# Pooled attention feeding a GELU MLP: v over 128 partitions, and a first batch by two head pairs

## The chip, the cores and the metric

The kernel runs on one core of a Trainium2 chip. The time is the device time of the program in microseconds, the median of several runs. The core's engines are TensorE (PE), VectorE (DVE), ScalarE (ACT), GpSimd (POOL) and SyncE (SP), each with its own instruction queue; SP, ACT and POOL issue transfers.

## The reference

Eight batches, eight heads, 576 positions of 64 columns. k and v are averaged over groups of eight positions (72 rows are left), and q attends to them; the result of all heads, 4608 rows of 512 columns, goes through two weight matrices with a tanh GELU between them. Everything is given and returned in f32.

```python
k_p = k.reshape(B, H, Sp, pool, D).mean(axis=3)          # Sp = 576 / 8 = 72
v_p = v.reshape(B, H, Sp, pool, D).mean(axis=3)
attn = softmax(scale * q @ k_p^T)
x = (attn @ v_p), heads side by side                     # (4608, 512)
out = gelu_tanh(x @ w_in) @ w_out                        # w_in (512, 2048), w_out (2048, 512)
```

## The kernel before, in words

The order of all instructions is written out by hand. The MLP works in nine groups `g` of 512 rows of x (`NG`), the attention in eight batches of 576 rows; while group g is worked on, batch `nb = g + 1` is prepared in the gaps. The work of one group has two parts.

In the first, `p1_mm` (L280) multiplies x by w_in: 16 blocks `fo` of 128 columns of the hidden layer, four matmuls `ko` each, 512 columns moving; `gelu` (L285) takes each block out of PSUM on ACT. `plan` (L369 and L372) says after which `fo` the preparation of batch nb is put: pooling of k (`k_steps`, three additions on DVE at L145), pooling of v (`v_steps`, by halves of four heads), the transposition of k on PE with its copies on DVE (`trans_k`, L168), and for batch 1 that of q (`trans_q`, L184). Later batches have q transposed by a DMA (`trans_q_dma`, L198).

In the second, `p2_mm` (L290) multiplies by w_out, 64 matmuls, and between them, at the positions `pos`, stands the attention of batch nb: `qk` (L208) makes scores with pooled positions on partitions, `expo` takes the exponential on ACT, `av` (L224) multiplies by pooled v. In `av` a weight tile holds 64 columns of v and 64 columns of the value 8, so that one matmul yields both the output and the sum of the softmax. `norm` (L241) makes the reciprocal as Exp(-Ln) on ACT, `mult` (L252) multiplies on DVE into `xT`. `store` (L294) copies a finished bank of output to SBUF on DVE and stores it from SP.

Group 0 has no group before it, so batch 0 is prepared and attended at the start, by itself (L305 to L348). There the sums of the softmax have matmuls of their own (`ones`, L234), and a unit of work is one pair of heads and one half `c` of the 576 positions: eight `av`, `norm` and `mult` in a row. Matmuls of `idle` (`spin`, L309) stand between the real ones. The first matmuls of group 0 are made early for the 288 columns of the first half (`early`, `take`), and completed later for the other 224.

Loads: k of batch 0 comes in two halves from SP and ACT, its last rows behind the second; v comes from SP by halves of heads, with pooled positions on 72 partitions (64 and 8). q, w_in, w_out and all later k and v are loaded by POOL, and q, w_in and w_out become bf16 on the way. w_in is loaded by four blocks of 512 columns, the first two at once, the others behind batch 1's k and q. `gate` (L358) is a copy on POOL that waits for a transposed q before later loads are issued. PSUM has eight banks, which `h_bank`, `o_bank` and the arguments `bank` share out.

Of the kernel before, what the change touches and what calls it, by code (L numbers as in the profile page):

```python
# [18 lines left out]
def kernel(  # L19
# [29 lines left out]
    kvp = ctx.enter_context(tc.tile_pool(name="kvp", bufs=2))  # L49
# [12 lines left out]
    vs, qs = {}, {}  # L62
    kts = [consts.tile([128, KR + 1, 512], F32, name=f"kt{i}") for i in range(2)]

    def load_k(b, engs):
        rows = k[b].rearrange("h (j l) d -> (h j) (l d)", l=8)
        main = rows[0:128 * KR].rearrange("(p r) c -> p r c", r=KR)
        n = KR // len(engs)
        for i, eng in enumerate(engs):
            eng.dma_start(out=kts[b % 2][:, i * n:(i + 1) * n], in_=main[:, i * n:(i + 1) * n])  # L70
        engs[-1].dma_start(out=kts[b % 2][64:128, KR], in_=rows[128 * KR:])

    def load_v(b, eng, h0=0, h1=H):
        if b not in vs:
            vs[b] = kvp.tile([Sp, H, 512], F32, name="vt")
        rows = v[b, h0:h1].rearrange("h (j l) d -> j h (l d)", l=8)

        for j0, j1 in ((0, 64), (64, Sp)) if eng is nc.sync else ((0, Sp),):
            eng.dma_start(out=vs[b][j0:j1, h0:h1], in_=rows[j0:j1])  # L79
# [8 lines left out]
    w_in_b = consts.tile([128, KO, DF], BF16, name="w_in_b")  # L88
    w_out_b = consts.tile([128, FO, DM], BF16, name="w_out_b")
    w_in_v = moe_w_in.rearrange("(ko p) f -> p ko f", p=128)  # L90
    w_out_v = moe_w_out.rearrange("(fo p) d -> p fo d", p=128)
# [4 lines left out]
    load_v(0, nc.sync, 0, 4)  # L96
    load_v(0, nc.sync, 4, 8)
# [4 lines left out]
    def load_w_in(i):  # L102
        nc.gpsimd.dma_start(out=w_in_b[:, :, i * 512:(i + 1) * 512], in_=w_in_v[:, :, i * 512:(i + 1) * 512])

    load_w_in(0)
    load_w_in(1)


    xT = consts.tile([128, KO, N], BF16, name="xT")

    kTs = [consts.tile([128, 2, H, Sp], BF16, name=f"kT{i}") for i in range(2)]
    kps = [consts.tile([128, KR + 2, D], BF16, name=f"kp{i}") for i in range(2)]

    vps = [consts.tile([Sp, PR, 2, 2, D], BF16, name=f"vp{i}") for i in range(2)]

    vz = consts.tile([Sp, PR, 2, 2, D], BF16, name="vz")
    ones = consts.tile([Sp, 2, 2, D], BF16, name="ones")
    gate = consts.tile([1, 2], BF16, name="gate")
# [4 lines left out]
    nc.vector.memset(kTs[0], 0.0)  # L123
    nc.vector.memset(vz, 0.0)
    nc.vector.memset(ones, 0.0)
    nc.vector.memset(ones[:, 0, 0], 8.0)
    nc.vector.memset(ones[:, 1, 1], 8.0)
    nc.gpsimd.memset(kTs[1], 0.0)
    nc.gpsimd.memset(kps[1], 0.0)
    nc.gpsimd.memset(kts[1][0:64, KR], 0.0)  # L130
    nc.gpsimd.memset(vps[0], 8.0)
    nc.gpsimd.memset(vps[1], 8.0)

    load_k(1, [nc.gpsimd])
    load_q(1)
    load_w_in(2)
    load_w_in(3)
    for i in range(4):
        nc.gpsimd.dma_start(out=w_out_b[:, 4 * i:4 * i + 4, :], in_=w_out_v[:, 4 * i:4 * i + 4, :])

# [13 lines left out]
    def v_steps(b, hf):  # L154
        t = vs[b][:, hf * 4:(hf + 1) * 4]

        def s3():
            w = (vps[b % 2] if b else vz)[:, 2 * hf:2 * hf + 2]
            for e in range(2):
                add(w[:, :, e, e, :], t[:, e::2, 0:64], t[:, e::2, 64:128])  # L160

        return [lambda: add(t[:, :, 0:256], t[:, :, 0:256], t[:, :, 256:512]),
                lambda: add(t[:, :, 0:128], t[:, :, 0:128], t[:, :, 128:256]), s3]
# [4 lines left out]
    def trans_k(b, bank, odd_eng=None):  # L168
        tp = half_bank(bank)[:, 0:(KR + 1) * 128].rearrange("p (r c) -> p r c", c=128)
        kf = kps[b % 2].rearrange("p r d -> p (r d)")  # L170
        for r in range(KR + 1):
            nc.tensor.transpose(out=tp[:, r, :], in_=kf[:, r * D:r * D + 128], identity=identb)  # L172
        tp = tp[0:D]
        n7 = (H - 1) * KH
        for e in range(2):
            copy = nc.scalar.copy if e and odd_eng is nc.scalar else nc.vector.tensor_copy
            o = kTs[b % 2][e * 64:(e + 1) * 64, e]
            copy(out=o[:, 0:H - 1].rearrange("p h (j r) -> p h j r", r=KR),  # L178
                 in_=tp[:, 0:KR, 0:n7].rearrange("p r (h j) -> p h j r", j=KH))
            copy(out=o[:, H - 1, 0:(128 - n7) * KR].rearrange("p (j r) -> p j r", r=KR),  # L180
                 in_=tp[:, 0:KR, n7:128].rearrange("p r j -> p j r"))
            copy(out=o[:, H - 1, (128 - n7) * KR:], in_=tp[:, KR, 64:128])

    def trans_q(b, i, t0, n, bank, eng):  # L184
        if b not in qTs:
            qTs[b] = bp.tile([128, 2, TP, 128], BF16, name="qT")
        tp = half_bank(bank)[:, 0:n * 128].rearrange("p (t c) -> p t c", c=128)
        for x in range(n):
            nc.tensor.transpose(out=half_bank(bank)[:, x * 128:(x + 1) * 128],  # L189
                                in_=qs[b][:, i, (t0 + x) * 128:(t0 + x + 1) * 128],  # L190
                                identity=identb)
        o = qTs[b][:, i, t0:t0 + n]
        if eng is nc.scalar:
            nc.scalar.copy(out=o, in_=tp)
        else:
            nc.vector.tensor_copy(out=o, in_=tp)

# [9 lines left out]

    def qk(b, c, pr, bank):  # L208
        for e in range(2):
            h = 2 * pr + e  # L210
            nc.tensor.matmul(out=PS[:Sp, bank + e, :CH].rearrange("j (t p) -> j t p", p=32),  # L211
                             lhsT=kTs[b % 2][:, c, h, :],
# [3 lines left out]
    def expo(b, c, pr, bank):  # L216
        e = ep.tile([Sp, 2, CH], BF16, name="e", bufs=8)
        nc.scalar.activation(out=e, in_=PS[:Sp, bank:bank + 2, :CH], func=ACT.Exp, scale=1.0 / 64.0)  # L218
        es[b, c, pr] = e

    def flat(w):
        return w.rearrange("j a d -> j (a d)")

    def av(b, c, pr, bank):  # L224

        e = es.pop((b, c, pr))
        for x in range(2):
            if b:  # L230
                nc.tensor.matmul(out=PS[:, bank + x, :CH], lhsT=flat(vps[b % 2][:, pr, x]),  # L231
                                 rhs=e[:, x, :], start=True, stop=True)
            else:
                for y in range(2):  # L234
                    w = vz[:, pr, y] if x else ones[:, y]
                    nc.tensor.matmul(out=PS[:, bank + 1 - x, :CH], lhsT=flat(w), rhs=e[:, y, :],  # L236
                                     start=(y == 0), stop=(y == 1))
# [3 lines left out]
    def norm(b, c, pr, bank):  # L241
        ld = ep.tile([128, CH], F32, name="ld")
        if b:
            nc.scalar.activation(out=ld[0:64], in_=PS[64:128, bank, :CH], func=ACT.Ln)  # L244
            nc.scalar.activation(out=ld[64:128], in_=PS[0:64, bank + 1, :CH], func=ACT.Ln)  # L245
        else:
            nc.scalar.activation(out=ld, in_=PS[:, bank + 1, :CH], func=ACT.Ln)  # L247
# [4 lines left out]
    def mult(b, c, pr, bank):  # L252
        rc = rcs.pop((b, c, pr))
        col = b * S + c * CH
        for x in range(2 if b else 1):
            rows = slice(x * 64, (x + 1) * 64) if b else slice(0, 128)
            nc.vector.tensor_tensor(out=xT[rows, pr, col:col + CH], in0=PS[rows, bank + x, :CH],  # L257
                                    in1=rc[rows], op=ALU.mult)

# [9 lines left out]
    def h_bank(g, fo):  # L269
        x, y = x_bank(g), 1 - x_bank(g)  # L270
        if fo == 4:
# [8 lines left out]
    def p1_mm(g, fo, ko, c0=0, c1=GROUP):  # L280
        r0 = g * GROUP
        nc.tensor.matmul(out=PS[:, h_bank(g, fo), c0:c1], lhsT=w_in_b[:, ko, fo * 128:(fo + 1) * 128],  # L282
# [22 lines left out]
    act_set(EXP_SET)  # L305
    for s in k_steps(0):
        s()

    def spin(n):  # L309

        for _ in range(n):
            nc.tensor.matmul(out=PS[:, 7, :], lhsT=idle[:, 0:128], rhs=idle, start=True, stop=True)  # L312

    def scores(b, c, pr, bank):
        qk(b, c, pr, bank)
        expo(b, c, pr, bank)

    spin(16)
    trans_q(0, *QG[0], 5, nc.scalar)
    trans_q(0, *QG[1], 6, nc.scalar)  # L320
    spin(4)
    trans_k(0, 4, nc.scalar)
    trans_q(0, *QG[2], 5, nc.vector)
    trans_q(0, *QG[3], 6, nc.vector)
    spin(2)
    for i, (c, pr) in enumerate(((0, 0), (0, 1), (1, 0), (1, 1), (0, 2), (0, 3), (1, 2), (1, 3))):
        if i:
            spin(1)
        scores(0, c, pr, (2, 0)[i % 2])
    for hf in range(2):  # L330
        for s in v_steps(0, hf):
            s()

    early = [(fo, ko) for ko in range(KO) for fo in range(4)]
    take = (0, 0, 0, 0, 0, 4, 6, 6)
    for i, (c, pr) in enumerate(ORDER):
        bank = (4, 6, 0, 2, 4, 6, 4, 6)[i]
        av(0, c, pr, bank)
        norm(0, c, pr, bank)
        mult(0, c, pr, bank)  # L340
        if i == 3:

            vs[1] = kvp.tile([Sp, H, 512], F32, name="vt")
            nc.vector.memset(vs[1][:, 0, 0:1], 0.0)  # L344
            load_v(1, nc.sync)
        for fo, ko in early[:take[i]]:
            p1_mm(0, fo, ko, 0, CH)
        early = early[take[i]:]  # L348


    for g in range(NG):
        nb = g + 1 if g + 1 < B else None
        act_set(GELU_SET)
        if g + 2 < B:
# [5 lines left out]
            load_v(g + 2, nc.gpsimd)  # L360
# [3 lines left out]
        if nb is not None:  # L364
            kk = k_steps(nb)
            v0, v1 = v_steps(nb, 0), v_steps(nb, 1)
            tk = [lambda: trans_k(nb, 4)]
            if g:
                plan = {2: kk[:1], 3: kk[1:], 7: v0[:1], 8: v0[1:], 9: tk, 11: v1[:1], 12: v1[1:]}  # L369
            else:  # L370
                tq = [lambda a=a, i=i: trans_q(nb, *a, 4 + i, nc.vector) for i, a in enumerate(QG)]
                plan = {0: kk, 4: tk, 6: tq[:1], 7: tq[1:2], 8: tq[2:3], 9: tq[3:], 10: v0, 12: v1}  # L372
# [5 lines left out]
        if g == 0:  # L378
            first = [(fo, ko, CH) for ko in range(KO) for fo in range(4)]
        else:  # L380
            late = 3
            rest = [fo for fo in range(4) if fo != late]
            first = [(fo, ko, 0) for ko in range(2) for fo in rest]
            first += [(late, 0, 0), (late, 1, 0)]
            first += [(fo, ko, 0) for ko in (2, 3) for fo in rest + [late]]
# [73 lines left out]
```

The softmax here doesn't subtract the row's maximum and nothing guards it: scores larger than these inputs give would overflow.

## Time and profile before

| | |
|---|---|
| median of 11 runs | 311.59 us (310.74 to 312.5) |
| the profiled execution | 311.74 us, span 310.0 us |
| mean granted TensorE clock | 0.992 |
| matmuls of `p1_mm` and `p2_mm` | 580 and 560 recorded, 375 and 379 ns each |
| exp of scores, 72x576 | 644 ns |
| Ln and Exp of `norm` in batch 0, 128x288 | 398 and 442 ns |
| HBM read, written | 36.70 MB, 9.44 MB |

The span is the time from the first to the last instruction of one profiled execution; around it lie the 1.7 us to its own time. Matmuls overlap, so the mean duration of one (379 ns) is not the distance between two: 31 of them follow each other in 6.94 us. A wait is put down to what ended it.

### The profile page before, as it was taken

The numbers are of one execution on the slowest core, as the hardware profiler recorded it, in microseconds if no ns is written. First come the engines' busy times: TensorE is split into PE (matmuls) and PEld (weight loads), VectorE is DVE, ScalarE is ACT, GpSimd is POOL, SyncE is SP. The second block draws the span as 40 slices with busy tenths as digits, with TensorE's granted clock in tenths as the row PEclk, the third lists the DMA queues.
The fourth block names the chain that finished last, engine by engine and source line by source line (L and its number), as shares of the span: only waits on it lengthen the run. The fifth ranks groups of instructions, "written<-read, shape, count | busy, mean of one in ns | idle before, by whom it ended". The sixth has DMA issues, their size and how long they took to land.

```text
span 310.0 us, 4249 instructions
## 1 busy us (share of the span) xinstructions
PE 297.1 (96%) x1516; PEld 150.3 (48%) x1545; DVE 157.2 (51%) x304; ACT 220.9 (71%) x414; POOL 30.8 (10%) x54
## 2 busy tenths in 40 slices
PE   6788999999999999999999999999999999999994
PEld 2455555445554455445544554455445544444441
DVE  3766636647668455854495358636772640020011
ACT  1686579877997799778987898689868987306500
POOL 8520000300201200030003000200000000000000
PEclk9988999999999999999999999999999999999998
DMA  7999995894995982588358826482101220121022
GB/s 225 236 279 248 185 193 116 271 220 83 261 220 113 239 183 63 112 232 174 79 110 226 188 71 95 164 184 71 41 0 33 49 56 0 36 68 34 2 68 69
DMA packets 32701, 41.05 MB, mean 132 GB/s; under 512 B 17608, under 2 KB 21704, under 8 KB 31784
## 3 DMA queue, kind: packets, MB, share of 16 engines
q0 software_dynamic: 10160, 24.26, 35.1%
q1 hardware_dynamic: 22200, 15.74, 21.7%
q10 hardware_dynamic: 320, 0.79, 0.8%
q8 instruction: 12, 0.20, 0.2%
q14 instruction: 9, 0.07, 0.1%
HBM read 36.70 MB, written 9.44 MB: 149 GB/s over the span
## 4 chain that ended last, share of the span: by engine, by line
PE 89%; DMA 4%; DVE 3%; ACT 1%; issue 1%; SPq 1%; DVEq 0%; ACTq 0%
PE PS L291 39%; PE PS L282 39%; PE PS L211 5%; PE PS L231 4%; DMA vt<-in_v_dram 4%; DVE kt L145 1%; PE PS L172 1%; SPq L79 1%; DVE vt L145 1%; DVE kT L178 0%; PE PS L236 0%; ACT rc L249 0%; PE PS L189 0%; ACT ld L247 0%; DVE osb L296 0%
## 5 line engine op out<-in xcount | busy, mean ns | idle before, releaser
L291 PE MATMUL PS<-w_out_b,gT 128*128 128x512 bf16 x560 | 133.7, 379 | 0.8
L282 PE MATMUL PS<-xT,w_in_b 128*128 128x512 bf16 (+2 forms) x580 | 129.2, 375 | 0.9 <-DVE vt L344 0.3
L288 ACT ACTIVATE gT<-PS 128x512 bf16<-128x512 f32 x144 | 81.3, 603 | 47.1 <-PE PS L282 46.9
L282 PEld LDWEIGHTS <-w_in_b 128*128 128x128 bf16 x592 | 57.7, 98 | 65.4 <-issue 2.0
L291 PEld LDWEIGHTS <-gT 128*128 128x128 bf16 x576 | 56.0, 97 | 56.9 <-issue 0.4
L296 DVE COPY osb<-PS 128x512 f32<-128x512 f32 x36 | 24.9, 692 | 94.9 <-PE PS L291 94.9
L257 DVE TENSOR_TENSOR xT<-PS,rc 64x288 bf16<-64x288 f32 (+1 forms) x120 | 54.5, 455 | 31.3 <-ACT rc L249 23.8
L218 ACT ACTIVATE e<-PS 72x576 bf16<-72x576 f32 x64 | 40.7, 644 | 8.0 <-PE PS L211 7.2
L145 DVE TENSOR_TENSOR vt<-vt 72x1024 f32<-72x1024 f32 (+1 forms) x32 | 30.5, 953 | 6.7 <-DMA vt<-in_v_dram 5.9
L249 ACT ACTIVATE rc<-ld 128x288 f32<-128x288 f32 x64 | 28.3, 443 | 2.6 <-DVE xT L257 0.6
L211 PE MATMUL PS<-qT,kT 128*72 128x288 bf16 x128 | 26.1, 286 | 0.4 <-ACT e L218 0.3
L244 ACT ACTIVATE ld<-PS 64x288 f32<-64x288 f32 x56 | 22.8, 407 | 1.3
L245 ACT ACTIVATE ld<-PS 64x288 f32<-64x288 f32 x56 | 22.5, 402 | 1.4
L263 ACT ACT_TABLE_LOAD x17 | 21.8, 1283 | 2.1 <-issue 1.8
L231 PE MATMUL PS<-e,vp 72*128 72x288 bf16 x112 | 23.1, 285 | 0.0
L211 PEld LDWEIGHTS <-kT 128*72 128x72 bf16 x128 | 14.4, 113 | 14.2 <-issue 1.4
L145 DVE TENSOR_TENSOR kt<-kt 128x1280 f32<-128x1280 f32 (+1 forms) x16 | 18.5, 1158 | 4.4 <-DMA kt<-in_k_dram 4.0
L358 POOL COPY gate<-qT 1x2 bf16<-1x2 bf16 x6 | 1.1, 176 | 155.0 <-DMA qT<-qb 155.0
L178 DVE COPY kT<-PS 64x504 bf16<-64x504 bf16 x15 | 10.1, 675 | 7.1 <-PE PS L172 7.0
L231 PEld LDWEIGHTS <-vp 72*128 72x128 bf16 x112 | 11.0, 98 | 3.3
L312 PE MATMUL PS<-idle 128*128 128x512 bf16 x28 | 9.0, 445 | 1.2 <-DVE idle L120 1.2
L145 DVE TENSOR_TENSOR vp<-vt 72x128 bf16<-72x128 f32 x28 | 6.9, 284 | 0.6
(45 smaller groups left out, 76.5 us busy)
## 6 DMA issues: line engine op xcount, KB each, us to landing
out_dram<-osb SPq DMA_DIRECT2D x142, 64.0 KB, 1.7
kt<-in_k_dram POOLq DMA_DIRECT2D x7, 1024.0 KB, 6.0
vt<-in_v_dram POOLq DMA_DIRECT2D x6, 1152.0 KB, 12.8
qb<-in_q_dram POOLq DMA_DIRECT2D x7, 576.0 KB, 15.3
w_in_b<-in_moe_w_in_dram POOLq DMA_DIRECT2D x4, 512.0 KB, 17.9
w_out_b<-in_moe_w_out_dram POOLq DMA_DIRECT2D x4, 512.0 KB, 24.5
vt<-in_v_dram SPq DMA_DIRECT2D x2, 512.0 KB, 11.1
vt<-in_v_dram SPq DMA_DIRECT2D x1, 1024.0 KB, 11.6
```

Of the source, the lines that this page charges most:

```text
L145: nc.vector.tensor_tensor(out=o, in0=a, in1=b, op=ALU.add)
L211: nc.tensor.matmul(out=PS[:Sp, bank + e, :CH].rearrange("j (t p) -> j t p", p=32), lhsT=kTs[b % 2][:, c, h, :], rhs=qTs[b][:, h // 4, :, h ...
L218: nc.scalar.activation(out=e, in_=PS[:Sp, bank:bank + 2, :CH], func=ACT.Exp, scale=1.0 / 64.0)
L231: nc.tensor.matmul(out=PS[:, bank + x, :CH], lhsT=flat(vps[b % 2][:, pr, x]), rhs=e[:, x, :], start=True, stop=True)
L244: nc.scalar.activation(out=ld[0:64], in_=PS[64:128, bank, :CH], func=ACT.Ln)
L245: nc.scalar.activation(out=ld[64:128], in_=PS[0:64, bank + 1, :CH], func=ACT.Ln)
L249: nc.scalar.activation(out=rc, in_=ld, func=ACT.Exp, scale=-1.0)
L257: nc.vector.tensor_tensor(out=xT[rows, pr, col:col + CH], in0=PS[rows, bank + x, :CH], in1=rc[rows], op=ALU.mult)
L282: nc.tensor.matmul(out=PS[:, h_bank(g, fo), c0:c1], lhsT=w_in_b[:, ko, fo * 128:(fo + 1) * 128], rhs=xT[:, ko, r0 + c0:r0 + c1], start=(ko ...
L288: nc.scalar.activation(out=gTs[g][:, fo, :], in_=PS[:, h_bank(g, fo), :], func=ACT.Gelu_apprx_tanh)
L291: nc.tensor.matmul(out=PS[:, o_bank(g, r), :], lhsT=gTs[g][:, fo, r * 128:(r + 1) * 128], rhs=w_out_b[:, fo, :], start=(fo == 0), stop=(fo ...
L296: nc.vector.tensor_copy(out=osb, in_=PS[:, o_bank(g, r), :])
```

## The change

All of it but the layout of v and of the weights lies in batch 0 and group 0.

- v of a batch is laid over 128 partitions: heads 0 to 3 on partitions 0 to 63, heads 4 to 7 on 64 to 127, and the eight last pooled positions of all heads in a fifth block of 64 partitions. `v_steps` adds all of it at once; the pooled last positions are moved to their partitions by two small DMAs from SP. Scores of heads 4 to 7 then have 128 rows (`pool_rows`), some of them empty, and `trans_k_copy` places k's columns to fit, with six copies for each parity of heads instead of three.
- v of batch 0 is loaded from SP and ACT. k's last rows are loaded by SP, and k's main columns are added ahead of them.
- Batch 0 makes the copies of k for heads 0 to 3 first, takes the scores of heads 0 to 3 after the first half of q, and shares q's evictions between ACT and DVE.
- `av0` and `norm0` work on two pairs of heads at once: four `Ln`, `Exp` and multiplications of 576 columns instead of eight of 288.
- The early matmuls of group 0 are of 512 columns, after the whole attention of batch 0.
- w_in is loaded in two blocks of 1024 columns, the first after `gate` has waited for q of batch 0. w_in and w_out are loaded by longer rows, and `p1_mm` reads every fourth column of w_in. Clearing of second buffers on POOL moves behind that.
- In group 0 the loads of batch 2 come after the gelus, the transposition of k stands at `fo` 6, of q at 10 to 13, v at 13. Later, all of v is added at `fo` 7 and 8; the matmuls of `ko` 2 move ahead of the last block's, and the last multiplication but one moves ahead of the last eviction.

```diff
-        engs[-1].dma_start(out=kts[b % 2][64:128, KR], in_=rows[128 * KR:])
+        engs[0].dma_start(out=kts[b % 2][64:128, KR], in_=rows[128 * KR:])
+    def load_v(b, engs):
+        rows = v[b].rearrange("h (j l) d -> j h (l d)", l=8)
+        t = vts[b % 2]
+        for i in range(2):
+            engs[-1].dma_start(out=t[32 * i:32 * i + 32, 4], in_=rows[64:, 4 * i:4 * i + 4])
+        for i in range(2):
+            engs[i % len(engs)].dma_start(out=t[64 * i:64 * i + 64, 0:4], in_=rows[0:64, 4 * i:4 * i + 4])
...
-    w_out_v = moe_w_out.rearrange("(fo p) d -> p fo d", p=128)
+    w_out_v = moe_w_out.rearrange("(q p j) d -> p q (j d)", p=128, j=4)
-    load_v(0, nc.sync, 0, 4)
-    load_v(0, nc.sync, 4, 8)
+    load_v(0, [nc.sync, nc.scalar])
...
+    nc.gpsimd.tensor_copy(out=gate, in_=qs[0][0:1, 1, 0:2])
     load_w_in(0)
-    load_w_in(1)
...
+        def pools(c):
+            add(t[:, c, 0:256], t[:, c, 0:256], t[:, c, 256:512])
+            add(t[:, c, 0:128], t[:, c, 0:128], t[:, c, 128:256])
+        def last():
+            add(vl, t[0:64, 4, 0:64], t[0:64, 4, 64:128])
+            for i in range(2):
+                nc.sync.dma_start(out=w[64 - 64 * i:72 - 64 * i, 4 * i:4 * i + 4], in_=vl[32 * i:32 * i + 32])
+        def main():
+            for i in range(2):
+                p = slice(64 * i, 64 * i + 64)
+                add(w[p, 4 * i:4 * i + 4], t[p, 0:4, 0:64], t[p, 0:4, 64:128])
...
+    def trans_k_copy(b, e, bank, lower=True, upper=True):
+        if lower:
+            heads(0, 4, 0, 0, KH)
+        if upper:
+            heads(4, H - 1, 64, 0, 16)
+            heads(4, H - 1, 0, 16, KH)
+            (three copies for the last head)
...
+    def av0(c, pr, bank):
+        for x in range(2):
+            (two matmuls with ones into bank + 2 + x, two with v into bank + x)
+    def norm0(c, pr, bank):
+        ld = ep.tile([128, 2, CH], F32, name="ld0", bufs=1)
+        nc.scalar.activation(out=ld, in_=PS[:, bank + 2:bank + 4, :CH], func=ACT.Ln)
+        rc = ep.tile([128, 2, CH], F32, name="rc0")
+        nc.scalar.activation(out=rc, in_=ld, func=ACT.Exp, scale=-1.0)
+        nc.vector.tensor_tensor(out=xT[:, pr:pr + 2, c * CH:(c + 1) * CH], in0=PS[:, bank:bank + 2, :CH],
+                                in1=rc, op=ALU.mult)
...
+        nc.tensor.matmul(out=PS[:, h_bank(g, fo), c0:c1], lhsT=w_in_b[fo // 8][:, ko, q * 512 + j:(q + 1) * 512:4],
...
+    spin(22, 1)
+    t = kts[0]
+    for r in (slice(0, KR), slice(KR, KR + 1)):
+        (k's three additions over r)
+    load_k(1, [nc.gpsimd])
+    load_w_in(1)
+    load_q(1)
+    (clearing of second buffers, then w_out)
...
+    av0(0, 0, 4)
+    norm0(0, 0, 4)
+    nc.vector.memset(vts[1][:, 0, 0:1], 0.0)
+    load_v(1, [nc.sync])
+    av0(1, 0, 0)
+    norm0(1, 0, 0)
+    spin(4, 6)
+    av0(0, 2, 4)
+    norm0(0, 2, 4)
+    av0(1, 2, 0)
+    norm0(1, 2, 0)
+    for fo, ko in early:
+        p1_mm(0, fo, ko)
...
-                plan = {0: kk, 4: tk, 6: tq[:1], 7: tq[1:2], 8: tq[2:3], 9: tq[3:], 10: v0, 12: v1}
+                plan = {0: kk, 6: tk, 10: tq[:1], 11: tq[1:2], 12: tq[2:3],
+                        13: tq[3:] + [lambda: pools(slice(0, 5)), last, main]}
...
-                    at(min(pos[i] + 9, 65), mult, *a)
+                    at(min(pos[i] + 9, 62 if i < len(ORDER) else 65), mult, *a)
```

## The prediction

> **What bounds the kernel now.** First the page: engines, and the chain that ended last.
>
> ```profile
> PE 297.1 (96%) x1516; PEld 150.3 (48%) x1545; DVE 157.2 (51%) x304; ACT 220.9 (71%) x414; POOL 30.8 (10%) x54
> ...
> PE 89%; DMA 4%; DVE 3%; ACT 1%; issue 1%; SPq 1%; DVEq 0%; ACTq 0%
> ```
>
> TensorE is 89% of the chain; the rest must be a start or an end. The windows view splits the span:
>
> ```profile
> 20.00:25.00 5.00, 4.73 (x26) 3.02 (x24) 2.29 (x6) 3.16 (x9) 1.44 (x2) 0.66 1.13 220
> ...
> 60.00:290.00 230.00, 228.73 (x1145) 114.04 (x1167) 119.58 (x229) 177.97 (x331) 13.83 (x24) 1.00 0.50 118
> ```
>
> From 60 to 290 us TensorE has 228.7 of 230 us: nothing is to be won there, only lost. At 20 to 25 us its clock is 0.66. Then the chain in order of time (start, us, what), and windows cut where the clock changes:
>
> ```profile
> 3.54 13.09 DMA vt<-in_v_dram
> ...
> 16.71 1.23 DVE vt L145
> ...
> 26.38 1.49 DVE kt L145
> ...
> 29.39 0.45 PE PS L172 x5
> ...
> 40.56 1.29 PE PS L291 x6
> ```
>
> ```profile
> 17.97:21.39 3.42, 2.10 (x15) 1.00 1.04 345
> 21.39:24.80 3.41, 3.40 (x15) 0.50 1.15 208
> ```
>
> The start waits for v until 16.6 us, then for v's additions and eight normalizations; after a gap TensorE runs at half clock from 21.4 to 24.8. The first output product starts at 40.4 us (its chain piece at 40.56). I count everything to that instant. Last, the transfers: windows whose last two columns are DMA share and GB/s, then tiles' and issues' landing times.
>
> ```profile
> 3.00:5.40 2.40, 2.40 (x10) 0.96 (x9) 0.36 (x4) 0.07 (x1) 2.40 (x4) 1.00 1.02 405
> ...
> 27.00:31.00 4.00, 2.99 (x21) 1.63 (x21) 3.29 (x7) 3.10 (x7) 0.00 (x0) 1.00 1.13 254
> 31.00:35.00 4.00, 3.93 (x30) 2.11 (x29) 1.98 (x6) 2.11 (x4) 0.00 (x0) 1.00 1.39 165
> ...
> 38.00:42.00 4.00, 4.00 (x21) 1.96 (x20) 2.81 (x6) 3.18 (x5) 0.00 (x0) 1.00 1.25 208
> ```
>
> ```profile
> w_out_b<-in_moe_w_out_dram POOLq DMA_DIRECT2D x4, 512.0 KB, 24.5
> ...
> qb<-in_q_dram POOLq DMA_DIRECT2D x2, 288.0 KB, 8.4
> ```
>
> The DMA engines are full from 3 to about 46 us. GB/s counts bytes as they land (41.05 MB in all, where 36.70 are read and 9.44 written), so a load that halves f32 to bf16 at 208 reads 416: full speed is 405 to 416 GB/s read everywhere. Needs are close behind: w_in's last quarter lands at 10.7 + 25.4 = 36.1 and is used at 37; w_out's last at 22.5 + 23.9 = 46.4, used at about 47.0. So there are two bounds at the start, the chain of small work and, about 1 us behind, the transfers.
>
> **The change, part by part.** *k's main columns first.* Before, the addition waits for all of k until 7.07 and pooled k is complete at 9.94. SyncE's main half landed at 0.75 + 5.2 = 5.95, so additions start near 6.1. Main part by the nearest shapes: 128x1024 1.22, 128x512 0.69, last step 0.42; tail 0.43 + 0.28 + 0.21 (the kp step of 320 columns took 0.49, v's of 128 0.28). End 9.3. Transposes and semaphores took 0.70 (9.94 to 10.64), then the lower copy 0.42 (504 columns 0.675, 288 here). q's first half, landed at 8.7 and now slowed to about 9.1 (below), is in time; its two evictions now go to ACT (0.69) and DVE (0.42). First exp 11.6 instead of 12.64.
>
> *Scores.* Eight exps at 0.576 are 4.6; between them stand q's second half and one ACT eviction (0.59) with a wait for it (about 0.5). The last exp ends near 17.5 (before 17.25). No gain by itself; the six copies of k where there were three (about 1.05 per head parity against 0.86) lie beside exps.
>
> *v.* Before, 1.22 + 0.70 + 2 x 0.28 for each half, behind a landing at 16.6. Now 128-partition adds: tail 0.7 + 0.2, main 1.22 + 0.69 + 2 x 0.42, after k's upper copies, ending near 17.0. The tail's sums then cross partitions in two small SyncE DMAs; no row shows one. Price: a 64 KB store lands in 1.7, a load in 5.2; nothing excludes either end. I take 2.3, near the store: landed by 15.7, covered by the exps. If a load's time, 18.5 and a stall of 1.5. TensorE's wait on v (1.2) goes.
>
> *Normalization by two pairs.* Before: eight Ln 0.40 and Exp 0.44, 17.14 to 25.97 with waits. Now four of 576 columns: Ln 0.62 (exp's 576 columns: 0.64), Exp 0.66, multiply 0.77. Walked through with two sets of four banks: Ln at 17.7, 18.95, 20.6, 21.85; multiplies end 19.75, 21.0, 22.65, 23.9. The early product needs the bank of the third: starts 22.7.
>
> *First product.* 64 matmuls at 0.216 = 13.8, transposes 1.3, small gaps 0.3: the output product could start at 38.1 instead of 40.4, **-2.3**. In this, 28.4 to 29.4, where TensorE waited for pooled k, is gone: k is added at fo 0, transposed at fo 6.
>
> *Clock.* Row: a window with 2.10 of 3.42 us busy was followed by half clock. The Trainium skill, "TensorE: Matmul & The Clock Gate", Part 1, gives an idle window of about 3.4 us as the condition. By the rule the new gaps (1.8 us before 9.5, later ones of 1 to 2) cost nothing; by the row any may cost up to half of 3.41, 1.7. The row decides that it is possible. The four `spin` matmuls (0.9) fill the window that failed; I put 0 in the sum and 1.7 in the upper bound.
>
> *The hold and the transfers.* v now goes on two queues (SyncE, ACT) beside q. v's 2 KB rows against q's 4.6 KB: q used to get about two thirds, now about half; at 400 GB/s q's second half lands at 12.0 (before 11.2), v at about 12.5. POOL then copies `gate` and issues w_in; queued behind it on POOL are the memsets of the second buffers, k, w_in's second half and q of batch 1, then w_out. Landing to issue was 0.55 for batch 2's gate (54.01 to 54.55); data flows 1.2 to 2.3 after, I take 1.65: the engines refill at 14.2, idle for 2.5. From there to the end of q1: w_in 4.19 + k1, v1, q1 at 1.18 = 7.73 MB. At 410 GB/s, 18.85: end 33.05. Landing trails the last packets by 1.15 (q: 10.0, 11.2): **34.2**. w_in's first half lands at 20.4 (needed 22.7). The second, with v1 beside it, at 31.05 (needed 29.9): TensorE waits. q1's first transpose stands after fo 10, at 32.7 unstalled; it waits until 34.2, **+1.5**. Then five blocks and transposes, 5.4: output product at 39.6.
>
> Rate: the row at 31 to 35 us has 165 GB/s while v's last eight partitions land; the new tail comes first, over 32 partitions. The Trainium skill, "DMA: Bandwidth & Descriptors", Rules for kernel authors, says transfers to disjoint partition halves bring nothing over one of 128 partitions. By that, v1, in halves still, goes on at the mixed rate of 27 to 31 us (254 landed, 350 read): its 3.2 MB with w_in then take 9.1 instead of 7.8, q1 lands at 35.5, and the sum is +0.6. I take 410, because the dip goes, which is the larger loss; the rule's value stays in the range.
>
> w_out ends at 44.4, last quarter needed 46.2. *v of batch 1* is added after q's last eviction: small DMA issued 6.7 after q1, needed 8.9 after: 2.2 against my 2.3, **+0.1**.
>
> *Queues.* ACT issues four DMAs (0.42 to 0.56 each) before its table load instead of two: 0, it idles to 9.27. SyncE issues v1 at 19.8 instead of 21.3, counted above. Batch 2's q, k and v move behind the gelus in the text: on POOL they follow w_out as before, on SyncE the q transpose follows v1's small DMAs, waiting for q2 anyway: 0.
>
> *Strided weights.* w_in is read every fourth column (8 bytes). No row shows a stride; an unstrided load takes 98 ns under a 216 ns matmul. Up to 2.2 times it costs 0, four times 101 us. A gain is excluded, it is hidden. I take 0.
>
> *Every later batch.* 128 rows instead of 72 cost nothing per matmul (286 and 285 ns whichever side has 72). DVE loses about 1.6 on v and gains 0.4 on k, unused: it is idle for half. The multiply moved ahead of the last eviction is at 58.2 instead of 59.3, eviction 0.5 later, and the block that uses its bank starts three matmuls (0.65) later: 0. In group 1, v2 landed at 68.6 and DVE waited 4.2; kT now ends 5.4 after v2 instead of 4.2, needed by 74.06 - 0.7. With v2 at 68.6 that costs 0.7; q2 and so v2 come about 1.9 earlier (w_out's end): 0. There the small DMA stands behind the q transpose on SyncE (landed 76.3, needed 76.3): 0 if that moves too, else 1.
>
> Sum: -2.3 + 1.5 + 0.1 = **-0.7** on 311.74 (span 310.0 and 1.74 around it), 311.04; the median of the runs is 0.15 lower: **310.9**.
>
> **Rivals.** *Transfers keep up* (0.28): w_in's second half by 29.9 and q1 by 32.7. For: fewer, larger rows. Against: k's 4 KB rows went no faster than w_out's 2 KB. 311.59 - 2.3: 309.2.
> *The hold starves TensorE* (0.22): q1 lands after 34.9, the break-even. From 14 to 47 us the kernel before read only about 370 GB/s; at that, 35.1, and landing up to 1.6 behind: 36.7, output product 42.1, +1.7: 313.3; a clock drop in the stall adds 1.7.
> *Strided weights* (0.02): over 216 ns; about 412.
> *Head no shorter* (0.08): q's second half or the small DMA takes what k's early sums give: 311.6.
> The likeliest (0.40) spans 310.2 to 311.6.
>
> **Numbers.** 0.2% is 0.62 us, about what a measurement of this kernel tells from none. Faster: 0.28 and 0.26 of the likeliest. Same: its other 0.14 and 0.08. Slower: 0.24. Range 309.0 to 312.9: leaves out half of the starving case, the strided one and the best tail.
>
> **What would show it.** First exp near 11.6; v no longer in the chain; clock 1.00 at 21 to 25 us; early product at 22.7; a TensorE wait on w_in near fo 8 or on q1 after fo 10; output product at 39.6. Wrong if that starts before 38.6 or after 40.4, if w_in's LDWEIGHTS exceed 200 ns, or if later groups stop being full.

## The result: slower by 1.1%, and the profile after

The median rises from 311.52 us (47 runs) to **314.42 us** (12 runs, 313.45 to 318.09). The ratio of the means is 1.0106, with a 95% interval of 1.0088 to 1.0125. The profiled execution took 315.69 us with a span of 313.9 us; the one of before 311.74 us and 310.0 us.

First the page of the changed kernel: its engines (busy us, share of the span, instructions) and the chain that ended last, by engine.

```profile
PE 298.0 (95%) x1502; PEld 157.5 (50%) x1531; DVE 150.6 (48%) x335; ACT 219.8 (70%) x403; POOL 41.1 (13%) x77
...
PE 88%; DMA 5%; DVE 3%; issue 1%; ACT 1%; DVEq 0%; SPq 0%; ACTq 0%
```

TensorE does the same work. Where the chain had 4% of DMA, it has 5%. Which transfers those are is read from the chain in order of time (start us, us, what):

```profile
0.75 5.63 DMA kt<-in_k_dram
...
12.59 0.30 DVE vt L139
13.16 5.56 DMA vz<-vl
18.86 0.40 PE PS L277 x2
...
24.71 0.81 PE PS L332 x3
...
40.31 0.84 DVE vt L139
41.45 5.45 DMA vp<-vl
47.03 0.41 PE PS L264 x2
```

The load of v is gone from the chain, as meant. In its place stand `vz<-vl` and `vp<-vl`, the pairs of small DMAs that `last` issues to bring the last eight pooled positions of v to their partitions. A pair moves 8 KB, and from its issue to the landing that TensorE needs pass 5.5 us. The waits view (us in total, times, longest) says what each cost:

```profile
POOL gate L109 <- DMA qb<-in_q_dram: 8.6, 1, 8.6
...
PE PS L264 <- DMA vp<-vl: 3.5, 1, 3.5
ACT ld L284 <- PE PS L264: 3.1, 1, 3.1
...
PE PS L277 <- DMA vz<-vl: 0.7, 1, 0.7
```

There is no wait of TensorE's matmuls for w_in or for q of batch 1 (issued at 15.26, landed 19.3 us later, just as TensorE came to it). The one large wait, 3.5 us, is that of the first `av` of batch 1, inside the second part of group 0. The timeline of TensorE gives the marks of the prediction (start, busy us):

```profile
24.71 6.20 PE L332 MATMUL PS<-xT,w_in_b 128*128 128x512 bf16 x27 [0.66 <-DVE xT L304]
...
39.91 1.46 PE L341 MATMUL PS<-w_out_b,gT 128*128 128x512 bf16 x6
...
43.17 0.41 PE L242 MATMUL PS<-qT,kT 128*72 128x288 bf16 x2
47.03 0.41 PE L264 MATMUL PS<-e,vp 72*128 72x288 bf16 x2 [3.45 <-DMA vp<-vl]
...
63.20 8.80 PE L332 MATMUL PS<-xT,w_in_b 128*128 128x512 bf16 x39
```

The output product starts at 39.91 (before 40.40). Its part of group 0 then runs until 63.20, 23.29 us, where it took 18.01 before (40.40 to 58.41). The windows view (length, then busy us of PE, PEld, DVE, ACT, POOL, then clock, DMA share, GB/s), cut where the clock changes:

```profile
10.90:14.31 3.41, 3.18 (x18) 2.45 (x19) 2.24 (x11) 2.01 (x4) 2.58 (x6) 0.50 0.63 93
...
43.40:47.00 3.60, 0.18 (x2) 0.00 (x0) 0.00 (x0) 0.65 (x1) 0.00 (x0) 1.00 0.82 153
45.04:48.45 3.41, 1.36 (x7) 0.80 (x9) 0.00 (x0) 1.04 (x3) 0.00 (x0) 1.00 0.34 62
48.45:51.86 3.41, 3.41 (x12) 1.44 (x11) 0.91 (x2) 2.11 (x5) 0.00 (x0) 0.50 0.95 180
...
90.00:290.00 200.00, 198.94 (x1000) 105.49 (x1019) 98.50 (x214) 154.86 (x290) 16.89 (x31) 1.00 0.44 105
```

From 43.4 to 47.0 TensorE does next to nothing, and from 48.45 to 51.86 it runs at half clock: a stall of 3.45 us and about half of 3.41 behind it. After that it is full again.

So the spans add up: output product reached 0.5 earlier, its part of group 0 longer by 5.3, the rest shorter by 0.9 (63.20 to 313.9 is 250.7 us; 58.41 to 310.0 was 251.6). -0.5 + 5.3 - 0.9 = +3.9, which is 313.9 against 310.0.

### The profile page after: what moved, and what is told of

It reads as the page before. It is cut to its first block, busy times and chain, and to the rows that moved or that the text cites. A ratio compares the mean times of both kernels' runs of the same rounds, so it can differ in the third digit from the quotient of the medians.

```text
span 313.9 us, 4326 instructions
## 1 busy us (share of the span) xinstructions
PE 298.0 (95%) x1502; PEld 157.5 (50%) x1531; DVE 150.6 (48%) x335; ACT 219.8 (70%) x403; POOL 41.1 (13%) x77
## 4 chain that ended last, share of the span: by engine, by line
PE 88%; DMA 5%; DVE 3%; issue 1%; ACT 1%; DVEq 0%; SPq 0%; ACTq 0%
PE PS L332 39%; PE PS L341 38%; PE PS L264 4%; PE PS L242 4%; DMA kt<-in_k_dram 2%; DMA vz<-vl 2%; DMA vp<-vl 2%; DVE vt L139 1%; DVE kt L139 1%; PE PS L177 1%; PE PS L207 1%; PE PS L277 0%; PE PS L274 0%; PE PS L358 0%; DVE xT L304 0%
## 5 line engine op out<-in xcount | busy, mean ns | idle before, releaser
L332 PE MATMUL PS<-xT,w_in_b 128*128 128x512 bf16 x563 | 126.9, 379 | 1.3 <-DVE xT L304 0.7
L295 DVE TENSOR_TENSOR xT<-PS,rc 64x288 bf16<-64x288 f32 x112 | 51.0, 455 | 36.2 <-ACT rc L287 33.9
L250 ACT ACTIVATE e<-PS 72x576 bf16<-72x576 f32 (+1 forms) x64 | 41.0, 646 | 11.9 <-PE PS L242 11.1
L242 PE MATMUL PS<-qT,kT 128*72 128x288 bf16 (+1 forms) x128 | 27.2, 297 | 2.0 <-ACT qT L217 1.9
L264 PE MATMUL PS<-e,vp 72*128 72x288 bf16 (+1 forms) x112 | 23.4, 289 | 3.5 <-DMA vp<-vl 3.5
L242 PEld LDWEIGHTS <-kT 128*72 128x72 bf16 (+1 forms) x128 | 13.8, 109 | 16.3 <-issue 2.0
L139 DVE TENSOR_TENSOR kt<-kt 128x1280 f32<-128x1280 f32 (+5 forms) x18 | 18.8, 1047 | 2.2 <-DMA kt<-in_k_dram 1.7
L139 DVE TENSOR_TENSOR vt<-vt 128x1280 f32<-128x1280 f32 (+5 forms) x18 | 18.8, 1043 | 0.3
L187 DVE COPY kT<-PS 64x288 bf16<-64x288 bf16 (+2 forms) x48 | 13.0, 319 | 6.1 <-PE PS L177 5.9
L264 PEld LDWEIGHTS <-vp 72*128 72x128 bf16 (+1 forms) x112 | 11.0, 99 | 7.6 <-issue 3.7
## 6 DMA issues: line engine op xcount, KB each, us to landing
w_out_b<-in_moe_w_out_dram POOLq DMA_DIRECT2D x4, 512.0 KB, 17.2
```

The lines of the kernel that those rows point to most:

```text
L139: nc.vector.tensor_tensor(out=o, in0=a, in1=b, op=ALU.add)
L242: nc.tensor.matmul(out=PS[:n, bank + e, :CH].rearrange("j (t p) -> j t p", p=32), lhsT=kTs[b % 2][c][:, h, :n], rhs=qTs[b][:, h // 4, :, h ...
L250: nc.scalar.activation(out=e[:n], in_=PS[:n, bank:bank + 2, :CH], func=ACT.Exp, scale=1.0 / 64.0)
L264: nc.tensor.matmul(out=PS[:, bank + x, :CH], lhsT=window(vps[b % 2][:n], 2 * pr + x), rhs=e[:n, x, :], start=True, stop=True)
```

## The experiments

The first theory: the small DMAs' price is the error; give them time and the loss goes. The rivals: the hold of w_in, the strided weights, or the half clock by itself. Each kernel is the changed one with the edit shown; ratios are to the kernel before, on the same chip.

**tail_early.** Batch 1's last rows are pooled and sent five blocks earlier.

```diff
-    plan = {0: kk, 6: tk, 10: tq[:1], 11: tq[1:2], 12: tq[2:3],
-            13: tq[3:] + [lambda: pools(slice(0, 5)), last, main]}
+    plan = {0: kk, 6: tk, 8: [lambda: pools(slice(4, 5)), last], 10: tq[:1], 11: tq[1:2], 12: tq[2:3],
+            13: tq[3:] + [lambda: pools(slice(0, 4)), main]}
```

> The changed kernel, with one thing moved: v's last pooled rows of batch 1 are added, and sent through their two small DMAs, after fo 8 of group 0 and not after fo 13; the rest of v stays at fo 13. Theory A (the two small DMAs land 5.5 us after their issue while the DMA engines are full, and the 3.5 us wait of the first av of batch 1 and the half clock behind it are what makes the change slower): the wait of 3.5 us and the half clock at 48.5 to 51.9 go, the second product of group 0 takes 18.0 instead of 23.4 us, about 5 us less than the changed kernel's profile, so about 309.5 to 310.5 and faster than the kernel before. The two DMAs, issued at about 33 us, still take 4 to 6 us to land. Theory B (the transfers held back are what costs, w_in and q of batch 1 come late): the time hardly moves, 313.5 to 314.5. Theory C (the many copies and additions on DVE delay the start): same as B.

Measured: 311.67 us, 1.0010 [0.9989, 1.0030], above the 309.5 to 310.5 expected. The wait for `vp` is gone, and group 0's second part takes 18.0 us again (41.06 to 59.06). The loss of 2.9 us is nearly all here. At one and the same mean clock, 0.999, the three such executions took 309.7 to 310.29 us and the one of the changed kernel 313.55, so the stall costs over 3 us without any half clock (the changed kernel has only this one such execution). What is left is batch 0's pair of copies; its waits view says:

```profile
PE PS L277 <- DMA vz<-vl: 2.1, 1, 2.1
```

They were issued at 12.69 and landed 5.86 later; a half clock from 20.49 to 23.90 followed, and the early product started only at 25.96.

**tail_early_no_hold.** The same, and the copy to `gate` ahead of w_in is taken out.

```diff
-    nc.gpsimd.tensor_copy(out=gate, in_=qs[0][0:1, 1, 0:2])
     load_w_in(0)
```

> As tail_early, and w_in's first half is issued at once, not after q of batch 0 has landed. Theory A with the transfers as the next bound: the DMA engines no longer stand idle from 12 to 14 us, w_in's second half and q1 land about 1.5 us earlier, but v of batch 0 lands later (w_in beside it); in tail_early the first product starts at 24.7, so transfers are not what it waits for: within 0.5 us of tail_early. Theory B (the hold is the cost): 1 to 2 us faster than tail_early. Theory D (the hold protects v and k of batch 0): v's sums end 1 to 2 us later, the same time slower.

Measured: 312.85 us, 1.0019 [1.0001, 1.0036]. No gain, with a median 1.2 higher than tail_early's (the intervals overlap): the pair of copies of batch 0 now took 6.14 us, TensorE waited 2.4 for it, and two periods of half clock followed (18.46 to 25.29). While the copies stand on the path, what an earlier w_in could give is hidden.

**rows_short.** The weights' layout goes back: adjacent columns of w_in, 2 KB rows of w_out.

```diff
-    w_out_v = moe_w_out.rearrange("(q p j) d -> p q (j d)", p=128, j=4)
+    w_out_v = moe_w_out.rearrange("(fo p) d -> p fo d", p=128)
...
-    lhsT=w_in_b[fo // 8][:, ko, q * 512 + j:(q + 1) * 512:4]
+    lhsT=w_in_b[fo // 8][:, ko, fo % 8 * 128:(fo % 8 + 1) * 128]
```

> The changed kernel with w_in's columns and w_out's rows in the order of before (adjacent columns as weights, w_out by 2 KB rows); the two halves of w_in stay. Theory A: weight loads of w_in fall from 113 to 98 ns, hidden beneath 216 ns matmuls, w_out lands within 1 us of before; time as the changed kernel, 314 to 314.8. Rival: strided weights cost TensorE time: 0.5 us or more faster.

Measured: 315.18 us, 1.0115 [1.0082, 1.0149], so the layout explains nothing of the loss. The groups of `w_in` weight loads (busy us, mean ns), of the changed kernel and of rows_short:

```profile
L332 PEld LDWEIGHTS <-w_in_b 128*128 128x128 bf16 x576 | 64.6, 113 | 57.6 <-issue 0.8
```

```profile
L332 PEld LDWEIGHTS <-w_in_b 128*128 128x128 bf16 x576 | 55.9, 98 | 66.0 <-issue 0.9
```

A step of 8 bytes costs 15 ns a load, under a matmul of 216. The longer rows of w_out landed no sooner: median 17.2 us after issue with them, 17.3 without.

**before_mult_62.** The kernel *before*, with nothing but the change's order at the end of a group, which stands in every group and not in group 0 alone.

```diff
-    first = [(fo, ko, 0) for ko in range(2) for fo in rest]
-    first += [(late, 0, 0), (late, 1, 0)]
-    first += [(fo, ko, 0) for ko in (2, 3) for fo in rest + [late]]
+    first = [(fo, ko, 0) for ko in range(3) for fo in rest]
+    first += [(late, ko, 0) for ko in range(3)]
+    first += [(fo, 3, 0) for fo in rest + [late]]
...
-    at(min(pos[i] + 9, 65), mult, *a)
+    at(min(pos[i] + 9, 62 if i < len(ORDER) else 65), mult, *a)
```

> The kernel before with one part of the change alone: the last multiplication but one stands ahead of the last eviction of the group, and the matmuls of ko 2 ahead of the last block. In the kernel before groups 1 to 3 take 32.12 us each and later ones 31.85; in the changed kernel all take 31.84. Theory: the late multiplication is what holds ko 3 in those three groups, so 3 x 0.27 = 0.8 us faster than before, about 310.7. Rival (the saving comes from DVE's smaller work on v): no change, 311.5.

Measured: 310.66 us, 0.9970 [0.9957, 0.9983]: 0.9 us won, by a step that the prediction had put at nothing. The timeline of VectorE at the end of group 1 shows why, first of before, then of the changed kernel:

```profile
91.45 1.88 DVE L257 TENSOR_TENSOR xT<-PS,rc 64x288 bf16<-64x288 f32 x4
```

```profile
94.82 0.94 DVE L295 TENSOR_TENSOR xT<-PS,rc 64x288 bf16<-64x288 f32 x2 [1.06 <-ACT rc L287]
...
96.52 0.92 DVE L295 TENSOR_TENSOR xT<-PS,rc 64x288 bf16<-64x288 f32 x2
```

Before, the last two pairs of multiplications ran back to back behind an eviction and ended at 92.4 and 93.33. The next group's first matmul had started at 90.53; by 92.26 (eight matmuls of 0.216) it could have come to those of `ko` 2, which read what the first of the two pairs writes, and four later to those of `ko` 3, which read the second. Groups 1 to 3 took 32.12 us each, where the changed kernel takes 31.84. There the last pair but one ends at 95.76 and the last at 97.44; the group starts at 95.04 and comes to `ko` 2 after six matmuls (96.33) and to `ko` 3 after twelve (97.63). Groups 4 to 6 took 31.85 before, too: with 576 rows in a batch and 512 in a group, only groups 1 to 3 read rows of the second half of the batch just attended.

**both_tails_early.** tail_early, and batch 0's last rows are pooled and sent right behind the transposition of k.

```diff
     trans_k_mm(0, 4)
+    pools(slice(4, 5))
+    last()
     trans_k_copy(0, 0, 4, upper=False)
...
-    pools(slice(4, 5))
-    last()
```

> As tail_early, and in batch 0 too v's last pooled rows are added right after k's last columns (about 9.3 us) and their two small DMAs go out near 10.3 instead of 12.7 us, ahead of w_in's data. Theory A: the wait of the first v matmul (2.1 us in tail_early, until 18.7) goes or shrinks to v's main additions (end near 17.0), and with it most half-clock periods at 20 to 24 us; the first product starts near 23.0 instead of 26.0, and the time is 1.5 to 3 us below tail_early: 309 to 310. If transfers are the next bound, TensorE shows a wait on w_in near fo 8 or on q1 after fo 10, and the gain stops at about 1.5. Theory C (DVE's order bounds the start): the additions only move k's copies back by 0.6 us, time as tail_early or slower.

Measured: 309.76 us, 0.9949 [0.9935, 0.9964]. No `av` waits for a copy now, and only now does the transfers' bound show:

```profile
11.61 1.17 PE L242 MATMUL PS<-qT,kT 128*72 128x288 bf16 x4 [1.41 <-DVE qT L219]
...
34.89 0.45 PE L207 MATMUL PS<-identb,qb 128*128 128x128 bf16 x5 [0.49 <-DMA qb<-in_q_dram]
```

The first line of this TensorE timeline is the price of the edit: the three tail additions (0.97 us, after a wait of 0.50 for v's last rows to land) stand ahead of q's eviction on VectorE, and the first scores wait for it. The second is the wait for q of batch 1, which lands at 34.84, 23.3 us after the hold ended.

**both_tails_spin.** Idle matmuls more (26 for 22 at the start, 5 for 1 between the scores), against the half clock.

```diff
-    spin(22, 1)
+    spin(26, 1)
...
-        spin(1, 7)
+        spin(1 if i else 5, 7)
```

> As both_tails_early, with 26 instead of 22 idle matmuls ahead of k's transposition and five instead of one in the wait for the eviction of q's third part. If half-clock periods in the start are a cost of their own, set off by those two gaps: no half clock before 25 us, narrower spread of the runs and 0.5 to 1.5 us faster than both_tails_early. Rival (the gaps are not what sets it off, or the chain on ACT and DVE hides the slow clock): no change.

Measured: 310.37 us, 0.9958 [0.9940, 0.9976]. The profiled execution had full clock until 307 us, its early product at 23.41 and its output product at 39.25, both about 1.0 ahead of both_tails_early's. Yet the median is not lower (the intervals overlap): executions with mean clocks of 0.999 and 1.0 took 309.35 to 310.69, and what parts these from each other is not shown.

**spin_in_wait.** The changed kernel with 16 idle matmuls ahead of the scores and the `av` that wait for `vp`, so that they fill the wait.

```diff
+            if g == 0 and m == 14:
+                spin(16, 6)
             p2_mm(g, r, fo)
```

> The changed kernel with 16 idle matmuls (about 3.45 us) in the wait of batch 1's first av, so that the wait stays and the clock's fall behind it should not come. Theory A, in two parts (3.5 us of wait and about 1.7 us of half clock after it): the clock stays at 1.00 from 48 to 52 us, the second product of group 0 takes 21.7 instead of 23.4 us and the time falls by about 1.5 us, to 312.5 to 313.2. Rival (the half clock has another cause, or costs nothing): as the changed kernel, 314 to 315.

Measured: 315.13 us, 1.0123 [1.0089, 1.0158]; a miss. In the profiled execution it did what it should: clock 1.00 from 45 to 55, group 0's second part 21.45 us instead of 23.29. But the half clock comes in some executions and not in others: those of the changed kernel have mean clocks from 0.984 to 0.999, and the one with 0.999 still took 313.55 us. So the stall of 3.45 us makes the loss, and the clock adds to it in some runs.

**tails_no_hold.** both_tails_early without the copy to `gate` ahead of w_in (the edit of tail_early_no_hold).

> As both_tails_early, with w_in's first half issued at once, not after q. There TensorE waited 0.5 us for q of batch 1 after fo 10, so the transfers are now the bound behind the start. If the hold's idle of the DMA engines (12 to 14 us) is what makes q1 late: that wait goes and the time falls by up to 0.5 us, to about 309.3. If w_in's data keeps v of batch 0 or the two small DMAs waiting (in tail_early_no_hold they landed 6.1 us after issue): a wait of 1 to 3 us at the first v matmul, and 310.5 to 312.

Measured: **308.34 us**, 0.9904 [0.9889, 0.9920], the fastest kernel of all, 3.0 us under before. TensorE's timeline:

```profile
22.72 6.20 PE L331 MATMUL PS<-xT,w_in_b 128*128 128x512 bf16 x28 [0.67 <-DVE xT L303]
...
32.49 0.44 PE L206 MATMUL PS<-identb,qb 128*128 128x128 bf16 x5
...
37.81 1.46 PE L340 MATMUL PS<-w_out_b,gT 128*128 128x512 bf16 x6
```

The early product starts at 22.72, q of batch 1 is waited for no more, and the output product starts at 37.81. That is the head which the prediction had forecast (22.7), without the hold that it took 1.5 us away for.

**tails_gate_half.** both_tails_early with `gate` on q's first half instead of the second.

```diff
-    nc.gpsimd.tensor_copy(out=gate, in_=qs[0][0:1, 1, 0:2])
+    nc.gpsimd.tensor_copy(out=gate, in_=qs[0][0:1, 0, 0:2])
```

> As both_tails_early, with w_in held until the first half of q has landed (about 9 us) instead of both. Data of w_in then flows from about 11.5, behind q's second half and beside the rest of v: q1 lands 1.5 to 2 us earlier, its wait of 0.5 us goes, first product unchanged at 24.5: 309.2 to 309.6. Rival: the small DMAs of batch 0, issued at 10.9, fall into the full engines and land after 16.5: 310.5 or more.

Measured: 308.85 us, 0.9928 [0.9909, 0.9948]; the output product at 38.15. Most of the hold's cost goes with its second half: the lowest of 14 runs, 308.43, is 0.12 above the lowest of tails_no_hold, and the intervals overlap.

**tails_order_gate_half.** The same, with batch 0's tail behind the first evictions, to take the wait of the first scores away (1.41 us in both_tails_early, 0.82 in tails_gate_half).

```diff
-    pools(slice(4, 5))
-    last()
     trans_k_copy(0, 0, 4, upper=False)
     trans_q(0, *QG[0], 5, nc.scalar)
     trans_q(0, *QG[1], 6, nc.vector)
+    pools(slice(4, 5))
+    last()
     trans_k_copy(0, 1, 4, upper=False)
```

> As tails_gate_half, with batch 0's last rows of v added behind the first three k and q evictions instead of ahead of them, so the first scores stand 1 us earlier and the small DMAs go out near 12.0. If issue before or after w_in's data fills the engines decides the landing: they land near 17.5 and the first v matmul waits 1 us, no gain over tails_gate_half, 309.2 to 310.5. If the evictions' delay is the larger part: first product at 23.5 and 308.5 to 309.2.

Measured: 311.04 us, 0.9969 [0.9935, 1.0002]; a miss. The copies were issued at 12.22 instead of 10.66; TensorE waited 1.2 for them, half clock followed at 19.43, and the early product came at 25.38 instead of 23.05. Ahead of q's eviction the additions delay the scores; behind it the copies come too late. The half clock is a large part of the price: the three of eight executions with mean clocks of 0.997 to 0.999 took 308.82 to 309.21.

**late_tail_full and late_tail_quiet.** Why do 8 KB take 5.5 us? The last two kernels change only the load. The first is tails_no_hold with batch 1's tail back at `fo` 13; the second adds a copy on POOL, ahead of the load of batch 2's q, that waits until DVE has written the pooled v.

```diff
+            if g == 0:
+                nc.gpsimd.tensor_copy(out=gate, in_=vps[1][0:1, 0, 0, 0:2])
             load_q(g + 2)
```

> tails_no_hold with batch 1's tail put back to fo 13, as in the changed kernel; only that differs. In the trace of tails_no_hold the q load of batch 2, issued by POOL at 21.9, is still landing until about 43. Copies would be issued near 39.4. Theory (the small copies wait behind what POOL's queue has put on the engines): first packets 3 to 4 us after issue, landing 5 us after, a wait of TensorE for vp of 2.5 to 3.5 us, median 308.3 + 3 = 311 (+1.7 in executions where a half clock follows). Rival (a 128-byte copy between partitions takes this long in itself, or SP is slow to start it): the same here; the two part in the next run.

> late_tail_full with one edit: the q load of batch 2, and behind it its k and v, are held on POOL until DVE has written the pooled v of batch 1, that is until just behind the issue of the copies. At their issue, near 39.4, only the last of w_out is left on the engines. Theory: packets begin 1.3 to 2 us after issue, the copies land 2 to 3 us after issue instead of 5, and TensorE's wait for vp is 0 to 0.8. Rival, the copy in itself: still 5.5, wait about 3. What the held loads cost batch 2 is not part of the question: k and v of batch 2 come some 3 us later and may stall group 1 by up to that; the median is then between 308.5 and 311.5 under the theory, 311 to 314 under the rival.

Measured: 313.68 us, 1.0074 [1.0043, 1.0105], and 309.45 us, 0.9931 [0.9909, 0.9952]. The chains, of late_tail_full and of late_tail_quiet:

```profile
39.89 5.22 DMA vp<-vl
45.11 0.14 issue
45.24 0.41 PE PS L263 x2
```

```profile
39.70 2.82 DMA vp<-vl
42.52 0.14 issue
42.66 0.40 PE PS L263 x2
```

The same instruction, issued within 0.2 us of the same time, takes 5.22 us with POOL's load in flight and 2.82 without. TensorE waits 3.2 and 0.8. The DMA views show the difference in the first 3.6 us of the one (39.89 to 43.5) and up to the landing of the other (39.70 to 42.6); q0 is POOL's queue, q1 carries the copies; packets, MB, share of 16 engines:

```profile
q0 software_dynamic: 270, 0.63, 90.9%
q1 hardware_dynamic: 21, 0.00, 0.5%
```

```profile
q0 software_dynamic: 66, 0.19, 52.0%
q1 hardware_dynamic: 40, 0.00, 1.2%
```

In the second, the 40 packets of the first copy (heads 0 to 3, which is all that the first `av` reads) move from 41.1 to 42.0, beginning 1.4 us after the issue. Its fellow, issued at 40.5, begins only at 43.2, when the q load that was let go at 40.54 is flowing. In the first kernel both begin at 43.3, 3.4 us after the first issue, as POOL's queue runs low. The rival, that such a copy takes this long in itself, is out. Batch 0 agrees: in both_tails_early its first copy is issued at 10.88, while the hold keeps w_in back, and its 40 packets move between 12.3 and 12.5, alone on the engines. With the 0.5 us from the last packet to the landing that late_tail_quiet shows (42.0 to 42.52), an estimate of its landing is 2.0 us after the issue.

In late_tail_full the two executions with a mean clock of 0.999 took 312.26 and 311.9 us, the four with 0.989 from 313.68 to 314.97, about 2 us more. The profiled executions of tail_early (0.994) and of the changed kernel (0.989) have one and two periods of half clock, so 0.989 stands for two. Where these lie in late_tail_full is not shown: its profiled execution, with 0.999, has none before its last microsecond.

Whether any other queue would have served the copies sooner was not tried.

## Why the prediction was wrong

**The steps that failed: *v* and *v of batch 1*.** The prediction had bounds for a small DMA of 1.7 (a store) and 5.2 us (a load), and took 2.3, near the store. The pairs took 5.56 and 5.45 in the changed kernel; the load's price was the right one. The price also isn't a constant: 2.82 where POOL's next load was held back (and about 2.0, by the estimate above, with nothing else on the engines), 5.22 to 6.14 where POOL's loads filled them. So 2.3 is the price of a quiet moment. The prediction had itself put the end of w_out's load at 44.4, behind the issue of batch 1's copies, and that line should have decided between its two ends. For batch 1 it wrote "needed 8.9 after" q, "2.2 against my 2.3, +0.1". The term measured +3.45, and the half clock from 48.45 came on top. Together group 0's second part is 5.28 longer where 0.1 was forecast; in tail_early all of that was gone (18.0 us again), and the ratio fell from 1.0106 to 1.0010.

**Batch 0's copies.** "Landed by 15.7, covered by the exps; if a load's time, 18.5 and a stall of 1.5." They landed at 18.72. TensorE waited 0.68, less than 1.5 because the head was late and TensorE itself came to them only at 18.18. In kernels with a quicker head the wait grew to 2.1 and 2.4.

**Clock.** The prediction put 0 into the sum and 1.7 into its upper end. The rule that it weighed, an idle window of 3.4 us (the Trainium skill, "TensorE: Matmul & The Clock Gate", Part 1), isn't enough for this trace: 1.36 of 3.41 us were busy in the window from 45.04 to 48.45, and half clock followed, as in the row of before with 2.10 of 3.42, where no gap was longer than 1.25. Nor does the busy share of a window decide: in late_tail_full, counted in steps of 3.41 us from its clock change at 6.13, the windows from 40.27 and from 43.68 were busy for 1.75 and 1.79, and full clock followed, behind a stall of 3.22 us. What decides stays open. The same section says that the window runs free of the kernel's start. The changed kernel's executions fit that, with mean clocks of 0.984 to 0.999. By the row, a stall of over 3 us should have carried the 1.7 in the forecast; but the stall was not foreseen.

***k's main columns first*, *Scores*, *Normalization by two pairs*, *First product*.** First exp at 11.82 (11.6 forecast); last exp ended at 18.61 (17.5); Ln at 19.55, 20.94, 22.50 and 23.90 (17.7 to 21.85), 1.85 to 2.05 later; the early product at the end of the third multiplication, as worked out, but at 24.71 instead of 22.7. From there to the output product 15.2 us, where 15.4 was forecast. Of the 2.0 us by which the early product was late, 1.1 were there by the last exp, behind the half clock from 10.90 to 14.31; the rest came behind the wait for the copies, which landed at 18.72. tails_no_hold, with neither, starts at 22.72.

***The hold and the transfers*.** The output product came at 39.91, near the 39.6 forecast, but by luck, not by the forecast's way: a head 2.0 later took the place of a wait of 1.5 for q, and no matmul waited for transfers. q of batch 1 landed at 34.53, where 34.2 was forecast, 0.05 ahead of its first transposition (34.58); in both_tails_early it landed at 34.84, with a wait of 0.49. Without the hold that kernel gains another 0.45% (ratios 0.9949 and 0.9904, intervals apart), about 1.4 us (the fastest executions of the two, 309.52 and 308.31, are 1.2 apart). So the hold's price was about right in size, though it was hidden behind a larger loss. The wait for q, by which the forecast had it, is only some 0.5 of it; why the early product starts sooner too without the hold (22.72, against 23.41 in both_tails_spin, both at full clock) is not shown. Of the two values weighed there, 34.2 was nearer to the changed kernel's 34.53 than the rule's 35.5.

***Strided weights*.** 113 ns instead of 98, hidden, as forecast.

***Every later batch*.** The multiply ahead of the eviction was put at 0 and is worth 0.9 (before_mult_62). The prediction costed it within its own group, and did not ask who waits for its result: the next group's matmuls. Its reading of 228.7 busy us of 230, that nothing was to be won there, failed by the overlap of matmuls: in the 2.00 us from 92.26, where the wait of 0.27 lies, TensorE counts as busy for 1.99. The changed kernel has that gain in it, and lost 2.9 all the same.

The rivals: none had the small DMA as a stall behind the output product's start. *The hold starves TensorE* gave 313.3 for another reason; its wait for q did not come. *Head no shorter* named "the small DMA takes what k's early sums give" and is what happened in the head, but it stopped there at 311.6. The range ended at 312.9. Two slips of its sums, 309.2 for 309.3 in *Transfers keep up* and 34.9 for 35.0 as the break-even, change nothing.

## What to carry to other kernels

A small transfer is priced by what is on the DMA engines when it is issued, not by its bytes: where the profile shows them full of a queue of large loads, take a load's time to landing and not a quiet store's, and put the issue that far ahead of its use. Ask for each such copy who waits at its end and whether the stall can bring a half clock; and price a moved instruction at whoever reads its result, in the next stage too. A cost that seems absent (here the hold) may only be covered by a larger one: after a fix, measure the other parts again.

## What the runs showed of the hardware

A full share of the DMA engines doesn't by itself say how long a small copy waits. In the changed kernel, batch 2's copies are issued at 72.51, behind SP's own transposition, whose packets fill the engines at that time. The DMA view of 72.4 to 73.6 us:

```profile
DMA packets 1002, 0.25 MB, mean 211 GB/s; under 512 B 1002, under 2 KB 1002, under 8 KB 1002
...
q1 hardware_dynamic: 1002, 0.25, 114.8%
```

The copies' first packets followed at 73.86, 1.35 us after the issue, as soon as the transposition's were through: the copies waited for what was left of it. At 41.45, beside POOL's loads of w_out and q on another queue, the first packets took 4.0 us to begin, until 45.4. What counts looks like the backlog of large loads ahead of the copy; no run here shows by what mechanism it holds back the packets of another queue.
